# Agent attention and a maxout layer on one core: 2900 operations listed in another order

## The chip, the core and the metric

The kernel runs on one core of one Trainium2 chip. A core has five engines that each run their own instruction stream in order: TensorE (PE in the profile; its weight loads are shown apart as PEld), VectorE (DVE), ScalarE (ACT), GpSimd (POOL) and SyncE (SP), which here issues the DMA transfers. The engines wait for each other through semaphores. The metric is the device time of one execution in microseconds (us).

## The reference

Four batches of 12544 tokens with 128 channels go through an attention over 49 "agents", and the result through a maxout layer of width 768:

```python
def _attn_ref(q, k, v, agents):            # q, k, v: 4 x 12544 x 128; agents: 4 x 49 x 128
    a2k = sm(agents, k)                    # sm: softmax of scale * a @ b.T
    agent_v = a2k @ v                      # 49 x 128 for each batch
    q2a = sm(q, agents)
    return q2a @ agent_v

def _moe_ref(x, w1, w2, w3, w_out):        # x: 50176 x 128; w1, w2, w3: 128 x 768
    h = np.maximum(np.maximum(x @ w1, x @ w2), x @ w3)
    return h @ w_out                       # w_out: 768 x 128
```

Inputs and output are float32; 78.7 MB are read and 25.7 MB are written.

## The kernel before

**What is computed, and how.** The maximum of the three products is rewritten as p1 + max(p2 - p1, max(p3 - p1, 0)) with differences of weights, so that two products have to be formed per slice, and p1 goes into a linear part. For each batch the softmax over the keys gives 49 weighted values (`avT`), and their products with the weight differences give a tile `G` of 49 rows per batch. A group of 1024 queries (there are 49 groups, `s` = 0 to 48; 12 for each batch and one with the rests) then needs: its transposed queries (`qt` on TensorE and `qe` on VectorE, or `qd`, a DMA transpose, for the groups in `TURNED`), its scores (`sc`, L541), their exponentials on ScalarE (`ex`, L547), and for each of six slices `f` of the width 768 two hidden products (`u` and `v`, L566). ScalarE applies a relu to `u` (`a`, L579) and VectorE takes the maximum with `v` (`x`, L582); for `f` = 4 both are in the same PSUM tile, and ScalarE does both steps (L573, L576). Two output tiles `o` = 0, 1 collect a linear part (`li`, L595) and six products (`p`, L604); VectorE scales them (`ov`, L611) and SP stores them (`st`).

**Keys and values.** Batch 0 is worked off first, in 12 pieces of the keys (`kl0.g`) and values (`vl0.g`): load, cast (`kc` on POOL, `vc` on ScalarE), turn on TensorE (`kt`), copy (`ke`), scores (`ks`), exponentials (`kx`), totals (`to`) and values (`kv`). When all are in, `rc0` and `nr0` form `avT`, and `gp`/`gv` the first `G`. No hidden product can start before. The pieces of batches 1 to 3 are spread over the query groups before them; their keys are turned by DMA transposes issued by SP (`kt1.g` to `kt3.g`, L462), as are the queries of `qd`.

**Who decides the order.** A function `graph` names 2900 operations with engine, tiles and predecessors. The text `ORDER` (from L662 on) lists all of them, in one line of words such as `u.3.5/2`: the operation and the slot of each new tile. Each engine executes its own operations in the order of this list; an operation also waits for the operations that it reads from and for the last user of the slot that it takes over. The number of slots is fixed: 3 for the hidden products (`UV`, two PSUM banks each), 2 for the smaller PSUM tiles (`OM`, one bank), 13 for loads (`LD`), 3 each for the casts `QB` and `KB` and the transposed `QT` and `KT`, 11 for outputs (`OS`). Ten `wm` operations (L390) are matmuls of the identity that nothing reads.

**Modes of TensorE.** `graph` gives each TensorE operation one of three modes: `u` and `v` run as two matmuls side by side on 49 rows each (ROW), `sc` and the `G` products as two on 64 columns each (COL), everything else on the full array (FULL):

```python
add(f"u.{s}.{f}", PE, em.hidden(s, f, C31, True), mm(...), mode=ROW, ...)
add(f"sc.{s}", PE, em.q_scores(s), mm(...), mode=COL, ...)
def add(self, name, eng, fn, cost, mode=FULL, ...)
```

In the list of before, after the first hidden product `u.0.1`, TensorE has 1479 operations, and 586 times the mode differs from that of the operation before.

Of the kernel before, what the change touches and what calls it, by code (L numbers as in the profile page):

```python
# [666 lines left out]
to0.6 ke0.9/2 kt0.11/0 ke0.11/0 ks0.11/0 kx0.11/2 vc0.0/0 vd0.11 to0.11 kv0.11 ke0.1/0 ks0.1/2 kx0.1/2 kt0.4/0 kl0.3/7 vl0.8/8
ke0.2/0 vl0.4/6 ks0.10/2 kv0.0 to0.1 vc0.9/0 ks0.9/1 kx0.9/0 kc0.8/2 ke0.4/1 kt0.8/0 vc0.6/1 vl0.3/10 sc.0/1 ke0.8/2 ks0.8/0
wm.2/1 to0.9 kv0.5 kv0.9 vl0.1/2 vc0.10/2 ks0.2/1 kx0.2/0 kx0.8/1 lw3a/9 lw1a/3 kv0.6 lw1b lw2a/12 lw3b lw2b ex.0/0 ks0.4/1
kc0.3/2 kt0.3/0 to0.8 ql.1/7 qc.1/0 lwo/0 cwo kx0.4/3 to0.4 to0.2 kv0.2 vc0.8/1 kx0.10/0 vc0.4/3 ke0.3/1 ks0.3/0 to0.10 kv0.8  # L670
# [213 lines left out]
```

## Time and profile before

| | us |
|---|---|
| median of 3 runs | 443.36 |
| lowest, highest | 443.36, 444.09 |
| span of the profiled execution | 440.9 |
| TensorE busy in the span | 421.0 |
| ScalarE busy | 392.4 |
| VectorE busy | 390.6 |
| GpSimd busy | 169.3 |
| issue to landing, loads of queries, keys, values (median) | 6.8, 8.3, 9.7 |

The profiled execution is told by its span, from the first to the last instruction, alone; the median of the runs is 2.5 us longer, which is what lies around the span. In the rows of the profile a line such as `L566` is a line of the kernel, the tile names stand as out<-in, and `x1248` counts instructions. A matmul's end is modelled, so starts are compared with starts below. "Idle" is the time that an engine had nothing running, and the name behind `<-` is what ended it. TensorE's granted clock was 0.999 over the span.

### The profile page before, as it was taken

The numbers are of one execution on the slowest core, as the hardware profiler recorded it, in microseconds if no ns is written. First come the engines' busy times: TensorE is split into PE (matmuls) and PEld (weight loads), VectorE is DVE, ScalarE is ACT, GpSimd is POOL, SyncE is SP. The second block draws the span as 40 slices with busy tenths as digits, with TensorE's granted clock in tenths as the row PEclk, the third lists the DMA queues.
The fourth block names the chain that finished last, engine by engine and source line by source line (L and its number), as shares of the span: only waits on it lengthen the run. The fifth ranks groups of instructions, "written<-read, shape, count | busy, mean of one in ns | idle before, by whom it ended". The sixth has DMA issues, their size and how long they took to land.

```text
span 440.9 us, 12824 instructions
## 1 busy us (share of the span) xinstructions
PE 421.0 (95%) x5246; PEld 268.6 (61%) x5246; DVE 390.6 (89%) x495; ACT 392.4 (89%) x461; POOL 169.3 (38%) x176
## 2 busy tenths in 40 slices
PE   2678999999999999999999999999999999999997
PEld 2564565666666665666666666665665655656676
DVE  2236998999999999999999989989999999999996
ACT  2269999999998999999999999999999999999983
POOL 3541556667295413480746345634403102000000
PEclk9999999999999999999999999999999999999999
DMA  8999999999999999999999999999987952462144
GB/s 323 409 410 384 347 297 335 315 390 266 399 352 239 297 316 352 273 279 307 419 410 259 242 279 381 268 290 304 277 253 214 246 138 76 117 207 58 49 165 173
DMA packets 99157, 122.50 MB, mean 278 GB/s; under 512 B 72535, under 2 KB 75291, under 8 KB 99099
## 3 DMA queue, kind: packets, MB, share of 16 engines
q1 hardware_dynamic: 98752, 121.46, 92.2%
q8 instruction: 41, 0.67, 0.6%
q10 hardware_dynamic: 347, 0.23, 0.2%
q14 instruction: 17, 0.14, 0.1%
HBM read 78.74 MB, written 25.69 MB: 237 GB/s over the span
## 4 chain that ended last, share of the span: by engine, by line
PE 74%; DMA 15%; ACT 3%; POOL 3%; SPq 2%; DVE 1%; issue 1%; DVEq 0%; ACTq 0%; POOLq 0%
PE UV L566 31%; PE OM L604 28%; DMA LD<-in_k_dram 8%; PE OM L595 5%; PE OM L541 3%; DMA LD<-in_q_dram 2%; ACT AS L579 2%; DMA LD<-in_moe_w_dram 2%; DMA LD<-in_v_dram 2%; PE OM L384 2%; PE OM L531 2%; PE OM L367 2%; DMA KT<-KB 1%; SPq L333 1%; POOL KB L343 1%
## 5 line engine op out<-in xcount | busy, mean ns | idle before, releaser
L582 DVE TENSOR_TENSOR R<-UV,AS 128x1024 bf16<-128x1024 f32 x245 | 293.1, 1218 | 17.2 <-PE UV L566 13.2
L579 ACT ACTIVATE AS<-UV 128x1024 bf16<-128x1024 f32 x245 | 246.1, 1025 | 16.9 <-PE UV L566 13.3
L566 PE MATMUL UV<-EQ,G 49*128 49x512 bf16 (+1 forms) x1248 | 182.6, 369 | 1.0 <-DVE G L456 0.2
L604 PE MATMUL OM<-wo_bf,R 128*128 128x128 bf16 x2340 | 178.3, 220 | 0.0
L604 PEld LDWEIGHTS <-R 128*128 128x128 bf16 x2352 | 139.3, 98 | 41.1 <-issue 38.6
L566 PEld LDWEIGHTS <-G 49*128 49x128 bf16 x1248 | 60.4, 93 | 63.6 <-issue 23.3
L525 POOL CAST QB<-LD 128x1024 bf16<-128x1024 f32 x49 | 50.6, 1043 | 113.4 <-DMA LD<-in_q_dram 73.5
L611 DVE TENSOR_TENSOR OS<-OM,RC 128x512 f32<-128x512 f32 x98 | 66.8, 681 | 3.0 <-PE OM L604 2.0
L343 POOL CAST KB<-LD 128x1152 bf16<-128x1152 f32 (+2 forms) x45 | 50.0, 1120 | 48.7 <-DMA LD<-in_k_dram 32.0
L573 ACT ACTIVATE UV<-UV 128x1024 f32<-128x1024 f32 x49 | 49.9, 1018 | 2.6 <-PE UV L566 1.6
L576 ACT ACTIVATE R<-UV 128x1024 bf16<-128x1024 f32 x49 | 50.2, 1024 | 1.4 <-PE UV L566 0.6
L343 POOL CAST VB<-LD 128x1152 bf16<-128x1152 f32 (+1 forms) x33 | 37.5, 1141 | 26.2 <-PE OM L553 13.6
L595 PE MATMUL OM<-G,EQ 128*128 128x256 bf16 x195 | 37.8, 275 | 0.0
L482 POOL TENSOR_TENSOR EA<-EA,EK 128x441 f32<-128x441 f32 x27 | 27.7, 1026 | 19.1 <-ACT EK L373 18.4
L547 ACT ACTIVATE EQ<-OM 128x512 bf16<-128x512 f32 x49 | 29.5, 603 | 1.2 <-PE OM L541 1.1
L355 DVE COPY KT<-UV 128x1152 bf16<-128x1152 bf16 (+1 forms) x12 | 8.3, 701 | 15.8 <-PE UV L350 13.5
L595 PEld LDWEIGHTS <-EQ 128*128 128x128 bf16 x196 | 12.3, 97 | 15.7 <-issue 15.2
L341 ACT ACTIVATE VB<-LD 128x1152 bf16<-128x1152 f32 (+1 forms) x12 | 12.3, 1040 | 9.9 <-DMA LD<-in_v_dram 9.6
L367 PEld LDWEIGHTS <-KT 128*128 128x128 bf16 x392 | 14.6, 98 | 9.1 <-issue 5.1
L541 PE MATMUL OM<-QT,agT 128*64 128x512 bf16 (+1 forms) x104 | 19.9, 388 | 0.0
L384 PEld LDWEIGHTS <-VB 128*128 128x128 bf16 x392 | 14.0, 96 | 7.3 <-issue 5.6
L373 ACT ACTIVATE EK<-OM 128x441 bf16<-128x441 f32 (+1 forms) x33 | 18.0, 546 | 0.4 <-PE OM L553 0.3
(71 smaller groups left out, 193.3 us busy)
## 6 DMA issues: line engine op xcount, KB each, us to landing
LD<-in_q_dram SPq DMA_DIRECT2D x48, 512.0 KB, 6.8
out_dram<-OS SPq DMA_DIRECT2D x48, 512.0 KB, 5.1
LD<-in_k_dram SPq DMA_DIRECT2D x40, 576.0 KB, 8.3
LD<-in_v_dram SPq DMA_DIRECT2D x40, 576.0 KB, 9.7
LD<-in_v_dram SPq DMA_DIRECT2D x3, 512.0 KB, 8.0
LD<-in_k_dram SPq DMA_DIRECT2D x3, 512.0 KB, 11.2
LD<-in_moe_w_dram SPq DMA_DIRECT2D x6, 192.0 KB, 8.6
KT<-KB SPq DMA_TRANSPOSE x33, 6.6
```

The costliest lines, as they stand in the source:

```text
L343: (self.nc.gpsimd if eng == POOL else self.nc.vector).tensor_copy(out=out, in_=src)
L525: return lambda: self.nc.gpsimd.tensor_copy(out=self.t[f"qb.{s}"], in_=self.t[f"q.{s}"][:, :GT, :])
L541: self.nc.tensor.matmul(self.t[f"qs.{s}"][h * H:(h + 1) * H, jj * P:(jj + pairs) * P], self.agT[:, b, :], self.t[f"qT.{s}"][:, 2 * jj + h: ...
L547: return lambda: self.nc.scalar.activation(self.t[f"e.{s}"], self.t[f"qs.{s}"], AF.Exp, scale=SCALE)
L566: self.nc.tensor.matmul(t[:, h, jj * P:(jj + pairs) * P], self.t[f"G{b}"][h * H:h * H + A, c + f * P:c + (f + 1) * P], self.t[f"e.{s}"][h ...
L573: return lambda: self.nc.scalar.activation(self.t[f"u.{s}.{f}"], self.t[f"u.{s}.{f}"], AF.Relu)
L576: return lambda: self.nc.scalar.activation(self.t[f"r.{s}.{f}"], self.t[f"u.{s}.{f}"], AF.Relu)
L579: return lambda: self.nc.scalar.activation(self.t[f"a.{s}.{f}"], self.t[f"u.{s}.{f}"], AF.Relu)
L582: return lambda: self.nc.vector.tensor_tensor(out=self.t[f"r.{s}.{f}"], in0=self.t[f"v.{s}.{f}"], in1=self.t[f"a.{s}.{f}"], op=ALU.max)
L595: self.nc.tensor.matmul(out[:, c:c + 2 * C], self.t[f"e.{s}"][:, j // 2 * P:(j // 2 + 1) * P], self.t[f"G{of[j // 2]}"][:, C1O:C1O + 2 * C ...
L604: self.nc.tensor.matmul(out[:, c:c + C], self.t[f"r.{s}.{f}"][:, j % 2, j // 2 * P:(j // 2 + 1) * P], self.wo_bf[:, f, :], start=False, st ...
L611: self.nc.vector.tensor_tensor(out=self.t[f"os.{s}"][:, j:j + n, :], in0=self.flat(f"o.{s}.{o}")[:, :n * C].rearrange("p (j c) -> p j c", ...
```

## The change

Only the text `ORDER` is replaced. The operations, their engines, tiles, slots and numbers stay; each engine issues as many instructions as before. What moves:

- **TensorE**: the same 1479 operations after `u.0.1`, in another interleaving of `u`, `v` and `p`; the mode now changes 605 times. The ten `wm` stand among the first 17 TensorE operations; they stood among the last 31 before `u.0.1`, but for one.
- **SP, start**: the loads of batch 0 come in another sequence. In both lists the same 24 loads of keys and values and one of queries (13.4 MB) stand ahead of the six loads of `w1`, `w2`, `w3`.
- **SP, later**: loads and DMA transposes are listed further ahead. Between a transpose of keys and the scores that read it stand, in the median, 81 TensorE operations where there were 19; for queries 81 where there were 40. Where a transpose stands so early, it takes over its slot right behind the last reader (`kt3.3` behind `ks3.0`). Some stores come later and in groups: six of them (`st.29` to `st.24`) now stand between `qd.42` and `qd.41`.
- **POOL**: casts of queries are listed right behind the transpose that frees their slot (`qc.31` behind `qd.27`).

```diff
 ORDER = """
-kl0.10/0 kc0.10/0 kl0.5/1 kl0.0/2 kc0.5/1 prep kt0.10/0 kt0.5/1 kc0.0/0 kt0.0/2 ke0.0/0 ke0.10/1 kl0.7/3 vl0.7/4 vc0.7/0 kl0.6/5
...
-wm.9/2 wm.6/1 kx0.3/1 to0.3 wm.1/0 su.0/1 re.0/0 wm.7/1 ql.2/6 qc.2/1 vd0.10 kv0.4 wm.4/1 rc0/0 vc0.3/1 d31a wm.3/0 vl1.0/5 kv0.3
-kv0.10 vc0.1/0 kv0.1 cw1 wm.8/0 nr0/0 gpa/0 gva wm.5/1 kl1.0/2 d21a kc1.0/2 gpc/2 gvc kl1.1/10 u.0.1/0 a.0.1/0 d31b d32 gpb/1 d21b
...
-sc.24/0 v.23.3/2 x.23.3/0 ex.24/0 v.23.1/1 u.23.2/0 x.23.1/4 a.23.2/1 li.22.1/1 p.22.1.5 kc3.0/0 kt3.0/1 ks3.0/0 kx3.0/1 p.22.1.0
...
-qc.41/2 qd.41/1 ql.47/8 p.38.0.3 p.38.0.1 ov.38.0/0 v.39.4 x.39.4/2 p.38.1.0 qc.47/2 v.39.5/1 x.39.5/9 u.40.1/0 a.40.1/0 p.38.1.4
...
+kl0.2/0 kl0.9/1 wm.0/0 kl0.0/2 ql.0/3 kl0.10/4 kl0.5/5 kc0.0/0 kc0.9/1 prep kt0.9/0 vl0.6/6 ke0.9/0 wm.7/1 wm.6/2 ks0.9/0
+kx0.9/0 wm.8/1 vl0.11/7 kl0.6/8 wm.5/2 vc0.11/0 qc.0/0 kc0.6/1 wm.3/1 wm.9/2 vl0.10/9 vc0.6/1 vc0.10/2 vd0.10 vl0.9/10 wm.1/0
...
+kx0.4/2 ks0.1/0 to0.4 kv0.4 kx0.1/0 vc0.3/3 vc0.1/2 to0.1 rc0/0 kv0.3 lw1a/12 kv0.1 lw3a/11 d31a lw1b cw1 nr0/0 gpa/0 gva lw2a/6
+d21a lw3b d31b lw2b d32 gpc/2 gvc u.0.1/0 a.0.1/0 gpb/1 ql.1/9 qc.1/0 d21b gpd/2 gvb u.0.5/1 a.0.5/1 gvd v.0.1/0 x.0.1/0 u.0.3/2
...
+p.22.0.3 ov.22.0/3 u.23.1/2 a.23.1/0 u.23.2/0 v.23.3/1 a.23.2/1 x.23.3/9 li.22.1/0 p.22.1.4 ks3.0/1 ql.30/3 qd.27/0 ql.31/11
+qc.31/2 kt3.3/2 p.22.1.2 qc.29/0 kc3.4/1 su.24 re.24/1 kx3.0/3 v.23.2/2 x.23.2/2 u.24.5/1 a.24.5/2 v.23.1/0 p.22.1.3 kv3.0
...
+x.38.0/2 li.37.1/1 p.37.1.3 p.37.1.5 u.39.2/2 st.31 st.35 st.32 st.36 st.24 a.39.2/1 v.38.1/0 x.38.1/10 p.37.1.2 u.39.0/1
...
+qd.41/0 v.38.3/0 x.38.3/8 st.34 st.37 li.38.1/0 p.38.1.5 u.39.4/2 a.39.4 v.40.2/1 x.40.2/6 u.39.5/0 p.38.1.4 a.39.5/0 p.38.0.3
...
 """
```

More of the change, by code (lines that the diff above doesn't have):

```diff
@@ L667 @@
[L667 to L670, printed above, removed]
@@ new lines @@
+vl2.7/2 su.13 u.13.3/0 v.12.2/1 x.12.2/0 p.11.1.1 kx2.1/2 qc.19/1 ea2.1 kv2.1 re.13/2 vc2.4/3 va2.1 u.12.0/2 p.11.1.2 a.13.3/2
+p.11.1.5 p.11.1.3 ov.11.1 a.12.0/0 u.13.4/0 a.13.4 v.12.0/1 x.12.0/1 u.13.5/2 li.12.0/1 qt.14/0 qe.14/2 a.13.5/1 p.12.0.3
+p.12.0.4 v.13.4 x.13.4/5 u.13.1/1 a.13.1/0 v.13.5/2 p.12.0.0 x.13.5/9 p.12.0.1 p.12.0.5 p.12.0.2 ov.12.0/7 sc.14/0 u.13.0/0
+v.13.3/2 x.13.3/7 ex.14/2 a.13.0/1 u.13.2/1 li.12.1/1 p.12.1.3 ks2.2/0 p.12.1.5 p.12.1.0 kx2.2/3 a.13.2/2 kt2.5/2 ql.20/12
@@ new lines @@
+va2.5 ov.15.1 a.16.0/1 u.17.4/0 a.17.4 v.16.2/2 x.16.2/0 u.17.5/1 a.17.5/2 ea2.4 vc2.8/2 vc2.10/3 kc2.10/2 ea2.5 li.16.0/0
+p.16.0.5 qt.18/1 qe.18/1 kt2.8/2 v.17.4 x.17.4/5 st.12 st.2 kl3.2/10 kl3.0/12 qc.22/2 kc3.0/0 v.16.0/2 x.16.0/6 p.16.0.2
+p.16.0.4 sc.18/1 v.17.5/1 x.17.5/7 ex.18/1 u.17.3/0 a.17.3/1 p.16.0.1 p.16.0.3 p.16.0.0 ov.16.0/6 u.17.2/2 a.17.2/0 v.17.3/0
+x.17.3/1 u.17.1/1 a.17.1/2 li.16.1/1 ks2.6/0 kx2.6/3 ea2.6 v.17.2/2 x.17.2/9 p.16.1.1 p.16.1.5 v.17.1/0 x.17.1/4 u.17.0/1
+a.17.0/1 su.18 kv2.6 re.18/1 kt2.9/0 va2.6 p.16.1.4 vc2.9/0 u.18.5/2 a.18.5/0 p.16.1.0 v.17.0/1 x.17.0/6 vl3.3/1 u.18.3/0
@@ new lines @@
+x.19.0/0 u.20.5/2 a.20.5/1 v.20.5/1 x.20.5/8 li.19.0/0 p.19.0.5 p.19.0.4 sc.21/1 ex.21/1 v.20.1/2 x.20.1/3 u.20.3/0 p.19.0.3
+p.19.0.0 p.19.0.2 a.20.3/2 u.21.3/1 p.19.0.1 ov.19.0/2 li.19.1/1 a.21.3/1 u.20.4/0 v.20.3/2 x.20.3/2 p.19.1.1 ks2.9/0 p.19.1.2
+a.20.4 kx2.9/3 ea2.9 fo2/0 u.20.2/1 a.20.2/0 v.20.4 x.20.4/6 su.21 kv2.9 vc3.0/0 kc3.5/2 vc3.2/2 qc.26/1 ql.29/10 ql.27/11
+qd.26/2 va2.9 p.19.1.3 re.21/1 v.20.2/2 x.20.2/7 u.20.0/1 p.19.1.5 p.19.1.4 li.20.0/0 p.19.1.0 ov.19.1 u.21.5/0 a.20.0/2
@@ new lines @@
+p.24.0.0 ks3.2/1 kx3.2/1 ea3.2 p.24.0.4 ov.24.0/9 u.25.2/1 a.25.2/0 v.25.3/2 v.25.4 x.25.4/3 x.25.3/8 kv3.2 va3.2 li.24.1/0
+p.24.1.0 v.25.2/1 x.25.2/1 p.24.1.2 u.25.0/2 a.25.0/2 v.25.1/0 su.26 re.26/0 p.24.1.3 u.26.5/1 a.26.5/0 li.25.0/1 x.25.1/2
+p.25.0.4 u.26.1/2 v.26.5/0 x.26.5/7 a.26.1/1 u.26.4/1 a.26.4 p.25.0.2 p.24.1.4 p.24.1.5 p.24.1.1 ov.24.1 u.26.3/2 a.26.3/0
+v.25.0/0 x.25.0/4 p.25.0.5 sc.27/0 ex.27/1 vc3.6/2 kt3.5/0 v.26.4 x.26.4/5 v.26.3/2 p.25.0.1 ks3.3/0 kx3.3/0 ea3.3 p.25.0.0
+x.26.3/6 p.25.0.3 ov.25.0/2 u.27.5/0 a.27.5/2 u.26.2/1 v.26.1/2 x.26.1/9 su.27 kv3.3 va3.3 re.27/1 vl3.7/3 vc3.7/1 li.25.1/1
@@ new lines @@
+st.15 x.28.1/5 u.28.2/1 a.28.2/1 li.27.1/1 p.27.1.5 qt.30/0 p.27.1.2 qe.30/0 u.29.3/2 a.29.3/0 v.28.0/0 x.28.0/4 p.27.1.3
+li.28.0/0 p.28.0.4 v.28.2/1 u.29.5/2 a.29.5/2 x.28.2/8 p.27.1.0 p.27.1.1 p.27.1.4 ov.27.1 p.28.0.1 v.29.5/0 u.29.4/2 a.29.4
+u.29.1/1 a.29.1/1 x.29.5/0 p.28.0.3 p.28.0.2 vc3.8/3 p.28.0.0 p.28.0.5 ov.28.0/7 sc.30/1 qd.33/0 ex.30/1 v.29.3/0 v.29.4
+x.29.4/1 x.29.3/6 v.29.1/1 x.29.1/10 ks3.6/0 su.30 li.28.1/1 p.28.1.3 kt3.9/2 kx3.6/2 u.29.0/0 a.29.0/0 u.30.3/2 a.30.3/1
+p.28.1.2 kv3.6 va3.6 re.30/1 p.28.1.1 v.29.0/1 x.29.0/5 u.29.2/0 p.28.1.5 li.29.0/0 p.28.1.0 p.28.1.4 a.29.2/2 v.29.2/2 x.29.2/2
@@ new lines @@
+v.32.4 a.32.5/1 x.32.4/3 v.32.5/2 x.32.5/8 u.32.1/0 a.32.1/0 p.31.0.0 p.31.0.2 p.31.0.5 ov.31.0/8 sc.33/1 u.32.2/1 v.32.1/2
+x.32.1/10 ex.33/1 v.32.2/0 a.32.2/1 x.32.2/4 li.31.1/0 p.31.1.0 p.31.1.1 p.31.1.4 ks3.9/1 kx3.9/2 p.31.1.2 u.33.5/1 a.33.5/0
+v.32.3/2 x.32.3/2 su.33 p.31.1.5 u.32.0/0 a.32.0/1 kv3.9 va3.9 re.33/0 p.31.1.3 ov.31.1 u.33.4/1 a.33.4 v.32.0/2 li.32.0/1
+p.32.0.2 p.32.0.5 x.32.0/5 v.33.5/0 x.33.5/0 st.11 ea3.9 fo3/0 v.33.4 x.33.4/1 p.32.0.3 u.33.3/2 a.33.3/1 p.32.0.4 p.32.0.1
@@ new lines @@
+a.41.0/2 u.40.4/2 a.40.4 p.39.0.2 qc.46/2 qc.44/0 qc.48/1 p.39.0.1 p.39.0.4 v.41.2/0 u.40.5/1 a.40.5/0 x.41.2/10 p.39.0.3
+p.39.0.0 ov.39.0/0 v.40.4 x.40.4/7 sc.42/0 st.28 qd.44/1 v.40.5/0 x.40.5/11 u.41.1/1 a.41.1/1 li.39.1/1 p.39.1.1 ex.42/2
+v.41.0/2 x.41.0/0 p.39.1.2 u.40.3/0 a.40.3/0 v.41.1/1 x.41.1/4 p.39.1.0 p.39.1.5 p.39.1.3 su.40/0 re.40/2 u.42.0/2 v.40.3/0
+x.40.3/2 p.39.1.4 ov.39.1 a.42.0/2 u.42.2/1 a.42.2/1 li.40.0/0 p.40.0.2 p.40.0.1 u.41.4/2 a.41.4 v.42.2/0 x.42.2/1 u.41.5/1
+a.41.5/0 p.40.0.3 p.40.0.0 su.41/1 re.41/1 p.40.0.5 p.40.0.4 ov.40.0/7 v.41.4 x.41.4/9 v.41.5/0 x.41.5/3 u.42.1/1 a.42.1/1
@@ new lines @@
+a.45.2/1 p.42.1.5 p.42.1.3 ov.42.1 qd.47/2 st.40 st.42 p.43.0.0 u.44.4/1 a.44.4 v.45.2/0 x.45.2/4 u.44.5/2 p.43.0.1 a.44.5/0
+p.43.0.2 su.44/0 re.44/0 p.43.0.4 p.43.0.3 ov.43.0/6 v.44.4 x.44.4/7 v.44.5/0 x.44.5/1 u.45.1/2 a.45.1/1 li.43.1/1 p.43.1.3
+p.43.1.4 v.45.0/1 x.45.0/3 sc.46/0 ex.46/1 u.44.3/0 a.44.3/0 v.45.1/2 x.45.1/6 p.43.1.5 p.43.1.0 su.45/0 p.43.1.1 re.45/2
+u.46.0/1 a.46.0/2 v.44.3/0 x.44.3/0 p.43.1.2 ov.43.1 u.46.2/2 a.46.2/1 li.44.0/0 p.44.0.2 p.44.0.5 u.45.4/1 a.45.4 v.46.2/0
+x.46.2/5 u.45.5/2 a.45.5/0 p.44.0.0 p.44.0.4 p.44.0.3 p.44.0.1 ov.44.0/3 v.45.4 x.45.4/2 v.45.5/0 st.38 x.45.5/10 li.44.1/1
@@ new lines @@
+p.44.1.1 u.46.1/2 a.46.1/1 sc.47/0 ex.47/0 v.46.0/1 x.46.0/11 p.44.1.5 u.45.3/0 a.45.3/0 v.46.1/2 x.46.1/1 st.43 p.44.1.4
+su.46/0 re.46/1 p.44.1.2 p.44.1.0 u.47.0/1 a.47.0/2 v.45.3/0 x.45.3/7 p.44.1.3 ov.44.1 u.47.2/2 a.47.2/1 li.45.0/0 p.45.0.4
+p.45.0.0 u.46.4/1 v.47.2/0 x.47.2/0 u.46.5/2 a.46.4 a.46.5/0 li.45.1/1 p.45.0.1 p.45.0.3 p.45.0.5 p.45.0.2 ov.45.0/6 v.46.4
+x.46.4/8 u.47.1/0 v.46.5/2 x.46.5/9 st.44 a.47.1/1 p.45.1.1 p.45.1.3 p.45.1.5 v.47.0/1 x.47.0/10 sc.48/0 ex.48/2 v.47.1/2
+x.47.1/6 u.46.3/0 a.46.3/0 p.45.1.4 li.46.0/0 p.46.0.4 p.45.1.2 p.45.1.0 u.47.5/0 a.47.5/2 u.48.2/1 ov.45.1 v.46.3/2 x.46.3/3
@@ L853 @@
+p.47.0.3 p.47.0.4 ov.47.0/3 a.48.4 v.48.4 a.48.3/2 v.48.3/1 x.48.3/5 p.47.1.0 p.47.1.1 x.48.4/8 li.48.0/0 p.48.0.1 p.48.0.2
+p.48.0.5 p.48.0.0 ov.47.1 st.47 p.48.0.4 p.48.0.3 ov.48.0/6 st.48.0 li.48.2/1 li.48.1/1 p.48.1.5 p.48.1.1 p.48.1.3 st.48.1
+p.48.1.2 p.48.1.4 p.48.1.0 ov.48.1 st.48.2 p.48.2.5 p.48.2.4 p.48.2.0 p.48.2.2 p.48.2.3 p.48.2.1 ov.48.2 st.48.3
 """
```

321 lines of the change are left out of this document (140 added, 181 removed).

## The prediction

> **What bounds the kernel now.** I read the page first, then busy time by stretch, then the starts of single matmuls in the timeline, and last the DMA rows. The page's span, TensorE's line and its chain of waits:
>
> ```profile
> span 440.9 us, 12824 instructions
> ...
> PE 421.0 (95%) x5246; PEld 268.6 (61%) x5246; DVE 390.6 (89%) x495; ACT 392.4 (89%) x461; POOL 169.3 (38%) x176
> ...
> PE 74%; DMA 15%; ACT 3%; POOL 3%; SPq 2%; DVE 1%; issue 1%; DVEq 0%; ACTq 0%; POOLq 0%
> ```
>
> The same busy times by stretch (columns: length, then PE, PEld, DVE, ACT, POOL busy with counts, clock, DMA share, GB/s):
>
> ```profile
> 0.00:10.00 10.00, 3.17 (x26) 2.32 (x26) 2.13 (x15) 1.28 (x1) 3.62 (x9) 1.00 0.84 313
> 10.00:20.00 10.00, 5.28 (x58) 3.89 (x59) 3.07 (x5) 3.41 (x6) 5.13 (x6) 1.00 1.03 410
> 20.00:30.00 10.00, 8.23 (x112) 6.57 (x110) 4.96 (x8) 5.69 (x8) 4.35 (x4) 1.00 1.02 409
> 30.00:40.00 10.00, 8.01 (x144) 5.28 (x144) 3.52 (x10) 9.25 (x14) 1.15 (x1) 1.00 1.04 394
> 60.00:430.00 370.00, 369.13 (x4562) 232.73 (x4559) 351.00 (x430) 349.30 (x406) 144.40 (x148) 1.00 0.93 268
> ```
>
> There are two stages. For 40 us batch 0 is loaded, at about 410 GB/s, and no compute engine is full. After that TensorE is busy for 369.13 of 370 us, while VectorE and ScalarE have 19 and 21 us free. A busy PE may hide waits, so the starts decide (first column: start):
>
> ```profile
> 260.38 1.15 PE L566 MATMUL UV<-EQ,G 49*128 49x512 bf16 x6
> 261.47 0.40 PE L604 MATMUL OM<-wo_bf,R 128*128 128x128 bf16 x4
> ...
> 264.14 1.07 PE L604 MATMUL OM<-wo_bf,R 128*128 128x128 bf16 x16
> 265.14 0.88 PE L566 MATMUL UV<-EQ,G 49*128 49x512 bf16 x6
> 265.95 0.84 PE L604 MATMUL OM<-wo_bf,R 128*128 128x128 bf16 x12
> 266.73 0.41 PE L541 MATMUL OM<-QT,agT 128*64 128x512 bf16 x2
> 267.07 0.88 PE L566 MATMUL UV<-EQ,G 49*128 49x512 bf16 x6
> 267.88 0.39 PE L595 MATMUL OM<-G,EQ 128*128 128x256 bf16 x2
> ...
> 268.44 0.61 PE L604 MATMUL OM<-wo_bf,R 128*128 128x128 bf16 x8
> 268.98 0.60 PE L566 MATMUL UV<-EQ,G 49*128 49x512 bf16 x4
> 269.52 0.62 PE L604 MATMUL OM<-wo_bf,R 128*128 128x128 bf16 x8
> ```
>
> From start to next start, 16, 12 and 8 matmuls of `p` take 1.00, 0.78 and 0.54 us. Four more cost 0.22 to 0.24, so a `p` operation is about 0.223 us and each of these runs has about 0.10 us on top (0.78 - 3 x 0.223 = 0.11; 0.54 - 2 x 0.223 = 0.09). That extra stands wherever the next operation has another mode. The back-to-back sequence shows no idle at all here: TensorE is the bound, and its time is its work plus mode changes plus what it really waits.
>
> It does wait a little. In the first row above six hidden matmuls took 1.09 us where 0.81 is usual. The rows of the two other engines at that place:
>
> ```profile
> 259.49 1.22 DVE L582 TENSOR_TENSOR R<-UV,AS 128x1024 bf16<-128x1024 f32 x1
> 260.07 1.02 ACT L576 ACTIVATE R<-UV 128x1024 bf16<-128x1024 f32 x1
> ```
>
> VectorE ended at 260.71 and ScalarE at 261.09, each releasing a `UV` slot that a hidden product was waiting for. Comparing all matmul starts with the usual step between the same two kinds of operation, I find 52 such waits of over 0.06 us, 7.4 us together; the first and the last are in these rows:
>
> ```profile
> 43.39 0.71 PE L566 MATMUL UV<-EQ,G 49*128 49x512 bf16 x4
> ...
> 416.30 1.02 PE L566 MATMUL UV<-EQ,G 49*128 49x512 bf16 x6
> ```
>
> **Part 1, mode changes.** The list of before changes mode 586 times after `u.0.1`, the new one 605 times: 19 more, at 0.10 us, +1.9 us. All of it is on the path, since TensorE has nothing to overlap it with. Bounds: the `sc` pair took 0.34 us (266.73 to 267.07), 0.12 above the 0.215 of its columns, so 19 x 0.12 = 2.3 above; below, 0.09 from the x8 run gives 1.7. I take 1.9. The matmuls themselves are the same 1479 operations, at zero.
>
> [...]
>
> **Part 2, waits for `UV` slots.** How long a slot is taken, from two pieces of the chain of waits in order of time (start, length), and what ScalarE and VectorE wait for in all (us, times, longest):
>
> ```profile
> 41.72 0.41 PE UV L566 x2
> 42.15 1.56 ACT AS L579 x2
> ```
>
> ```profile
> DVE R L582 <- PE UV L566: 12.9, 34, 0.7
> ACT AS L579 <- PE UV L566: 12.6, 40, 0.6
> ```
>
> ScalarE starts 0.43 us after the product, so a slot that ScalarE frees is back after 0.43 + 1.02 = 1.45 us, one that VectorE frees after 0.43 + 1.22 = 1.65. I counted, with the durations above, how much TensorE work is listed between a product and the next user of its slot. Too short are 21 slots behind ScalarE and 18 behind VectorE in the old list, 4.9 us missing altogether; in the new one 21 and 16, 4.8 us. So -0.1. The rest, 7.4 - 4.9 = 2.5 us, comes from queues on the two engines: the share of stretches of 10 us in which an engine is given more than 10 us of work is 23% for ScalarE and 30% for VectorE before, 21% and 32% after, and the mean overload of the two together falls from 0.22 to 0.19 us. Scaled, -0.3. Together -0.4. Bounds: all 2.5 us gone (-2.6), or as much again (+2.4).
>
> **Part 3, the start.**
>
> ```profile
> 31.17 8.14 DMA LD<-in_moe_w_dram
> ...
> 36.30 2.23 ACT L341 ACTIVATE VB<-LD 128x1152 bf16<-128x1152 f32 x2
> 38.90 0.84 ACT L410 ACTIVATE w_bf<-LD 128x768 bf16<-128x768 f32 x1 [0.37 <-DMA LD<-in_moe_w_dram]
> ...
> 40.27 0.39 PE L566 MATMUL UV<-EQ,G 49*128 49x512 bf16 x2
> ```
>
> The last cast of values ends at 38.53 and the first hidden product follows at 40.27; a load of `w` issued at 31.17 lands only at 39.31. Both lists put the same 13.4 MB ahead of `w`, in one queue that is already full, so no sequence of them ends earlier unless the queue runs better: 30 to 40 us at 410 in place of 394 GB/s would give 10 x 16/410 = -0.4. Against that, the new list waits for slots in other places (13 `LD` slots, three `KB`); one load held up costs its own share of the queue, 0.59 MB/410 GB/s = +1.4. I take 0, since the loads that need an old slot have it freed by casts well before their turn in the queue. The warm-up matmuls at 0.38 us each lay in TensorE's free time (8.01 of 10 us busy at 30 to 40) and cost nothing there; nothing comes from their move, as the clock column is 1.00 from the first stretch on, where they hardly ran. The end of the list has the same dependencies in both (`u.48` to `ov.48.2`), at zero.
>
> **Part 4, transposes, loads, stores, casts.** Rows of the DMA issues and of POOL's longest wait behind a transpose:
>
> ```profile
> out_dram<-OS SPq DMA_DIRECT2D x48, 512.0 KB, 5.1
> ...
> KT<-KB SPq DMA_TRANSPOSE x33, 6.6
> ...
> QT<-QB SPq DMA_TRANSPOSE x29, 5.3
> ...
> POOL QB L525 <- DMA QT<-QB: 32.2, 8, 9.2
> ```
>
> In the old list the median transpose of keys stands 19 TensorE operations ahead of its reader, about 5 us; in the new one 81, about 20 us, against 6.6 us to landing. That is safer, but TensorE had hardly a wait for a transpose to lose, so it is worth 0. SP now stands behind `ks` and `sc` for `KT` and `QT` slots, with loads queued behind it, and POOL behind transposes (it did so for 32.2 us before, at no cost). Loads have a median of 194 TensorE operations to the scores that need them, so this is hidden too. The tightest place is `qd.41`: it needs the slot that `sc.40` frees, and six stores stand just ahead of it in SP's queue, 6 x 0.52 MB/410 GB/s = 7.7 us of transfers. `sc.39`, which lets SP go on, and `sc.41`, which reads the result, are 14 us of TensorE work apart; less 7.7 for the stores and some 5.3 for the two transposes this leaves about 1 us. At zero, with +2 as the upper end.
>
> **Sum.** 440.9 + 1.9 - 0.4 + 0 + 0 = 442.4 us of span. With the 2.5 us by which the median of the runs exceeds the profiled span, 444.9; I say 444.8, 0.3% above 443.36.
>
> **Rivals.**
> - *The slot waits shrink more than the modes cost (faster).* One mechanism: the new interleaving of `u`, `v` and `p` keeps ScalarE and VectorE from queueing behind each other, so that TensorE's 7.4 us of slot waits fall. For it: both engines have 5% free, and the overload of VectorE falls from 0.110 to 0.086 us per stretch. Against it: the number of too short slots is equal in both lists. It decides once waits fall by more than 1.9 + 0.9 = 2.8 us, to under 4.6. With the waits halved and the better queue of part 3: 443.36 + 1.9 - 3.7 - 0.4 = 441.2.
> - *Nothing that can be told.* The extra modes fall at places where TensorE would have waited for a slot anyway. Half of the 1.9 us would have to lie there: 443.36 + 0.9 - 0.4 = 443.9. For it speaks that waits and changes both cluster around the hidden products; against, that 52 waits are few beside 605 changes.
> - *Supply becomes the bound (slower by more).* SP, held behind `sc` for a `QT` slot, and the stores behind it make `qd.41` and its neighbours late. It begins where the 1 us of part 4 is used up; two or three such places at 2 us each give 444.8 + 2 to 6, about 448. Against it: 20 us of lead elsewhere.
> - *The order makes more of the queues on ScalarE and VectorE (slower)*: waits grow by the 2.4 us of part 2, 447.2; this is the upper end of the forecast's own range.
>
> **How the numbers follow.** What a measurement of this kernel can tell from no change is 0.2%, 0.9 us. Chances: forecast, modes paid and waits about as before, 0.46; waits shrink, 0.25; nothing to tell, 0.21; supply, 0.08. Slower by over 0.2% is the forecast and supply, 0.54; same 0.21; faster 0.25. The forecast's own range is 444.3 to 447.2. The whole range reaches down into the faster case, to 441.2, which leaves out about 0.09, and up to 447.3, which leaves out most of supply and a little more, about 0.1.
>
> **What would show it.** Right: runs of `p` and `u` in the timeline with the same steps but more of them alternating, TensorE busy for all but some us from 41 us on, idle of L579 and L582 behind `PE UV L566` between 50 and 430 us not under the 12.6 and 12.9 us of part 2, the first hidden product between 39.9 and 41.7. What would make the prediction wrong: steps at mode changes well under 0.10, slot waits under 4.6 us, a first hidden product before 39.5, or TensorE waiting for `QT`, `KT` or a cast.

## The result, and the profile after

The changed kernel takes 446.96 us (median; 446.09 to 448.31) against 443.63 us for the kernel before on the same chip: a ratio of 1.0073, 95% interval 1.0051 to 1.0096. It is slower by 3.3 us where the forecast had 1.4. The profiled execution has a span of 444.6 us against 440.9. The page of after, with the clock line of its 40 slices:

```profile
span 444.6 us, 12850 instructions
...
PE 421.9 (95%) x5246; PEld 265.8 (60%) x5246; DVE 391.8 (88%) x495; ACT 392.6 (88%) x461; POOL 169.2 (38%) x176
...
PEclk9988899999999999999999999999999999999999
...
PE 85%; ACT 5%; DVE 4%; DMA 3%; issue 2%; POOL 1%; SPq 0%; ACTq 0%; DVEq 0%; POOLq 0%
```

The busy times look like those of before. The clock line does not: TensorE's clock is cut in the third to fifth slice. By stretch (columns as in the prediction; the clock is the third number from the end), after:

```profile
20.00:30.00 10.00, 6.47 (x108) 5.10 (x106) 2.71 (x7) 6.99 (x11) 3.94 (x4) 0.87 1.02 410
30.00:40.00 10.00, 7.46 (x156) 6.01 (x154) 5.57 (x10) 7.95 (x11) 2.29 (x2) 0.95 1.03 395
38.00:41.00 3.00, 1.62 (x24) 0.93 (x24) 2.44 (x9) 2.60 (x5) 0.00 (x0) 1.00 1.09 371
41.00:48.00 7.00, 6.66 (x40) 2.79 (x38) 5.05 (x7) 4.71 (x7) 4.05 (x4) 0.51 1.03 400
60.00:430.00 370.00, 369.05 (x4550) 230.44 (x4547) 351.02 (x426) 348.42 (x406) 143.43 (x146) 1.00 0.93 266
```

and before, for the two stretches that the prediction had not looked at:

```profile
38.00:41.00 3.00, 2.59 (x33) 1.17 (x31) 2.88 (x9) 2.51 (x5) 0.00 (x0) 1.00 1.10 370
41.00:48.00 7.00, 6.51 (x62) 3.52 (x60) 6.69 (x9) 6.60 (x10) 3.64 (x4) 1.00 1.03 402
```

From 41 to 48 us TensorE is busy for 6.66 and 6.51 of the 7 us, but after has 40 matmuls there and before 62, at a granted clock of 0.51 in place of 1.00. Just ahead of it, from 38 to 41 us, TensorE was busy for 1.62 us after and 2.59 us before; that is where the warm-up matmuls stood. From 60 to 430 us the clock is 1.00, and after starts 12 matmuls fewer in the same time.

Where the 3.5 us by which TensorE ends later come from can be summed from the starts. For each kind of TensorE operation I took the usual time to the next start (with and without a change of mode; the value that 15% of its steps lie below, over the traces of the table) and called the rest excess. Times in us; the kernels below the first two are those of the experiments; the columns and the last operation's 0.3 add up to TensorE's end:

| kernel | mode changes | first hidden product | usual steps | excess up to 60 us | excess later | TensorE's end |
|---|---|---|---|---|---|---|
| before | 586 | 40.27 | 379.39 | 1.50 | 16.37 | 437.80 |
| after | 605 | 40.88 | 381.85 | 2.85 | 15.41 | 441.26 |
| w_both | 605 | 40.35 | 381.16 | 2.16 | 15.92 | 439.87 |
| h_ab | 585 | 40.91 | 379.92 | 2.93 | 17.29 | 441.34 |
| x1_more_modes | 624 | 42.45 | 382.99 | 1.32 | 16.92 | 443.96 |
| x2_fewer_modes | 533 | 40.97 | 374.40 | 2.58 | 47.83 | 466.05 |
| fewer_waits | 587 | 40.66 | 379.62 | 1.84 | 24.12 | 446.52 |
| banks_kept | 590 | 40.59 | 380.55 | 1.55 | 16.71 | 439.68 |

After against before: the first product +0.61; up to 60 us, at half the clock, +1.35 of excess and +0.69 in usual steps (five operations that occur only there, which the column takes as they ran: 381.85 against 381.16 in w_both); mode changes +1.77; waits later -0.96. Together +3.46.

The steps at mode changes are those of before. Timeline of after (first column: start):

```profile
264.79 0.61 PE L604 MATMUL OM<-wo_bf,R 128*128 128x128 bf16 x8
265.33 0.93 PE L566 MATMUL UV<-EQ,G 49*128 49x512 bf16 x6
266.20 1.07 PE L604 MATMUL OM<-wo_bf,R 128*128 128x128 bf16 x16
267.20 0.95 PE L566 MATMUL UV<-EQ,G 49*128 49x512 bf16 x6
```

Eight matmuls of `p` and a change take 0.54 us, sixteen and a change 1.00, as before.

### The profile page after: what moved, and what is told of

It is laid out like the page before. It is cut to its first block, busy times and chain, and to the rows that moved or that the text cites. A ratio compares the mean times of both kernels' runs of the same rounds, so it can differ in the third digit from the quotient of the medians.

```text
span 444.6 us, 12850 instructions
## 1 busy us (share of the span) xinstructions
PE 421.9 (95%) x5246; PEld 265.8 (60%) x5246; DVE 391.8 (88%) x495; ACT 392.6 (88%) x461; POOL 169.2 (38%) x176
## 4 chain that ended last, share of the span: by engine, by line
PE 85%; ACT 5%; DVE 4%; DMA 3%; issue 2%; POOL 1%; SPq 0%; ACTq 0%; DVEq 0%; POOLq 0%
PE UV L566 34%; PE OM L604 31%; PE OM L595 6%; PE OM L541 4%; PE OM L384 2%; DVE R L582 2%; DMA LD<-in_k_dram 2%; PE OM L531 2%; ACT AS L579 2%; PE OM L367 2%; PE OM L553 1%; ACT VB L341 1%; DMA ag_st<-in_agents_dram 1%; PE UV L350 1%; ACT EK L373 1%
## 5 line engine op out<-in xcount | busy, mean ns | idle before, releaser
L582 DVE TENSOR_TENSOR R<-UV,AS 128x1024 bf16<-128x1024 f32 x245 | 293.5, 1219 | 18.3 <-PE UV L566 12.9
L579 ACT ACTIVATE AS<-UV 128x1024 bf16<-128x1024 f32 x245 | 245.7, 1026 | 18.1 <-PE UV L566 15.4
L566 PE MATMUL UV<-EQ,G 49*128 49x512 bf16 (+1 forms) x1248 | 185.0, 371 | 1.3 <-DVE G L456 0.3
L604 PE MATMUL OM<-wo_bf,R 128*128 128x128 bf16 x2340 | 181.5, 220 | 0.0
L566 PEld LDWEIGHTS <-G 49*128 49x128 bf16 x1248 | 58.8, 93 | 64.7 <-issue 24.4
L373 ACT ACTIVATE EK<-UV 128x441 bf16<-128x441 f32 (+1 forms) x12 | 5.9, 504 | 15.2 <-PE UV L367 15.1
L384 PE MATMUL OM<-EK,VB 128*128 128x49 bf16 x392 | 17.7, 186 | 1.4 <-DVE KR L431 0.7
L373 ACT ACTIVATE EK<-OM 128x441 bf16<-128x441 f32 (+1 forms) x33 | 18.0, 547 | 0.9 <-PE OM L367 0.6
```

Of the source, the lines that this page charges most:

```text
L384: self.nc.tensor.matmul(out, vb[:, j, :], e[:, j * A:(j + 1) * A], start=False, stop=True, skip_group_check=True)
L566: self.nc.tensor.matmul(t[:, h, jj * P:(jj + pairs) * P], self.t[f"G{b}"][h * H:h * H + A, c + f * P:c + (f + 1) * P], self.t[f"e.{s}"][h ...
L579: return lambda: self.nc.scalar.activation(self.t[f"a.{s}.{f}"], self.t[f"u.{s}.{f}"], AF.Relu)
L582: return lambda: self.nc.vector.tensor_tensor(out=self.t[f"r.{s}.{f}"], in0=self.t[f"v.{s}.{f}"], in1=self.t[f"a.{s}.{f}"], op=ALU.max)
L604: self.nc.tensor.matmul(out[:, c:c + C], self.t[f"r.{s}.{f}"][:, j % 2, j // 2 * P:(j // 2 + 1) * P], self.wo_bf[:, f, :], start=False, st ...
```

## The experiments

**Warm-ups moved back (e1_warm_back) and moved away (e2_warm_front).** The first is after with eight of its `wm` back between `kv0.4` and `gpc`; the second is before with eight of its `wm` among the first operations:

```diff
 e1_warm_back, from after
-kx0.9/0 wm.8/1 vl0.11/7 kl0.6/8 wm.5/2 ...
-... to0.4 kv0.4 kx0.1/0 vc0.3/3 vc0.1/2 to0.1 rc0/0 kv0.3 lw1a/12 kv0.1
+... to0.4 kv0.4 wm.9/1 wm.6/2 kx0.1/0 vc0.3/3 vc0.1/2 to0.1 wm.1/1 wm.7/2 wm.4/1 rc0/0 kv0.3 wm.3/2 lw1a/12 kv0.1 wm.8/1
 e2_warm_front, from before
-prep kt0.10/0 kt0.5/1 kc0.0/0 kt0.0/2 ke0.0/0 ke0.10/1
+prep wm.9/1 wm.6/2 wm.1/1 kt0.10/0 kt0.5/1 wm.7/2 kc0.0/0 kt0.0/2 ke0.0/0 ke0.10/1 wm.4/2 wm.3/0 wm.8/2 wm.5/0
```

> The order of after, with eight of its ten warm-up matmuls taken from the first 17 TensorE operations and listed again between kv0.4 and gpc, where TensorE waits for the last values. Theory A (the warm-ups' move costs clock): the granted clock, 0.50 from 41.2 to 48.0 us in after, stays at 1.00 there; 25 fewer matmuls were started from 41 to 48 us than before, at some 0.085 us each about 2.1 us, so the time falls from 447.0 to about 444.9. Theory B (the clock was low where TensorE waited for other engines anyway, and mode changes and slot waits make up the whole 3.3 us): the time stays within 0.5 us of 447.0, whatever the clock.

> The order of before, with eight of its warm-up matmuls taken from ahead of the first hidden product and listed among the first TensorE operations, between prep and kt0.6. Theory A: the clock falls to about 0.5 for one or two pieces of 3 to 7 us near 40 us, and the time rises from 443.6 to between 444.5 and 446. Theory B: no more than 0.4 us above 443.6, even if the clock falls. If the clock stays at 1.00 here, TensorE's other work in these 10 us suffices and the warm-ups alone are not the cause in after.

Measured: e1_warm_back 444.77 us against 443.23 (ratio 1.0047, 1.0027 to 1.0067), e2_warm_front 445.03 against 443.23 (1.0043, 1.0029 to 1.0056). The stretch from 40 to 50 us of e1_warm_back, and that of e2_warm_front:

```profile
40.00:50.00 10.00, 9.32 (x83) 4.44 (x84) 9.36 (x14) 9.59 (x14) 5.38 (x6) 1.00 1.05 396
```

```profile
40.00:50.00 10.00, 9.14 (x62) 4.07 (x59) 7.71 (x13) 7.54 (x12) 5.26 (x6) 0.66 1.03 399
```

The eight matmuls, which nothing reads, decide the clock in both directions, and with it 1.8 us each way. Theory A holds, theory B falls. The price is somewhat under the 2.1 us expected, an estimate that had counted 25 fewer matmuls from 41 to 48 us where the two rows above show 22; at its own 0.085 us each that is 1.9.

But single executions of e1_warm_back lay between 443.8 and 452.4 us. The profile of a late execution of e1_ab, a variant of it with the later order of before, points to the reason.

**The two halves exchanged (h_ba, h_ab, e1_ab).** Three lists join one order up to `u.2.2` (61 us in before, 64 in after; the expectations had put it at 57) with the other behind it; operations that the first part lacks come at the joint.

```diff
 h_ba: before up to u.2.2, then after
 ... x.2.1/8
-u.2.2/2 v.2.3/1 li.1.1/1 vc1.1/2 kv1.1 ...
+kt1.1/0 ks1.1/0 su.2 kx1.1/0 kl1.3/4 ql.4/1 qc.4/2 kc1.3/2 vc1.1/1 ...
 h_ab: after up to u.2.2, then before   (e1_ab: the same behind e1_warm_back)
 ... qc.5/1 kx1.1/1
-u.2.2/1 v.2.3/2 li.1.1/0 kx1.1/3 ea1.1 kv1.1 p.1.1.0 ...
+u.2.2/1 v.2.3/2 li.1.1/0 kv1.1 p.1.1.1 a.2.2/0 ...
```

> The order of before up to u.2.2 (some 57 us), then the rest in the order of after: 606 mode changes after u.0.1 in place of 586, with the clock and the start of before. Theory A (modes at 0.10 us, slot waits about equal): 20 x 0.10 = +2.0, bounds 1.2 to 2.2 with the waits, so 444.8 to 445.8 against 443.6. Theory C (the start and the clock are the whole loss): 443.4 to 444.0.

> The order of after up to u.2.2, then the rest in the order of before: 585 mode changes after u.0.1, one fewer than before, with the start of after. Theory A: the first hidden product comes 0.6 us later than before and half a clock costs 2.1 us, so 443.6 + 2.7 - 0.1 = 446.2, at least 445.2. Theory B: 443.5 to 444.3, the start lost nothing.

> The order of e1_warm_back up to u.2.2, then the rest in the order of before: 585 mode changes in place of 605, same start and same clock as e1_warm_back. Theory A (what e1_warm_back still loses to before, 1.5 us, is mode changes): 444.8 - 20 x 0.096 = 442.9, at most 443.6. Theory D (it is the start, a later first product): no change from 444.8, at least 444.3.

Measured: h_ab 446.63 us against 443.23 (1.0088, 1.0067 to 1.0108), near the 446.2 of theory A, so theory B falls: with the start of after, and one mode change fewer than before, it is as slow as after. Its clock is that of after:

```profile
41.00:48.00 7.00, 6.66 (x40) 2.79 (x40) 5.08 (x7) 4.64 (x7) 4.06 (x4) 0.51 1.03 399
```

By the table the 20 fewer mode changes save it 1.93 us against after, and later waits take 1.88 back; behind another start the order of before waits more than in its own place (17.29 against 16.37 us). So this run alone would not show the price of the mode changes; x1_more_modes below does. The other join, h_ba, took 448.02 us, more than any theory had. Its timeline shows an accident of the joint:

```profile
61.96 0.39 PE L595 MATMUL OM<-G,EQ 128*128 128x256 bf16 x2
64.53 0.41 PE L384 MATMUL OM<-EK,VB 128*128 128x49 bf16 x9 [2.18 <-POOL VB L343]
```

POOL had been given the casts of `q.4` and `k1.3`, just loaded, ahead of the values that `kv1.1` needs; TensorE waited for 2.18 us, and then ran at half clock (0.50) from 65.1 to 68.6 us as well. Less the wait it would take 445.8 us, and less half of those 3.4 us as well 444.1; this estimate spans both theories, so the run is no clean test of the mode changes. It does show the forecast's supply rival in action, only not in the kernel that was forecast.

e1_ab took 445.46 us (1.0061, 1.0033 to 1.0088), with 12 executions from 443.96 to 452.01; its lowest is no lower than the 443.84 of e1_warm_back, so 20 fewer mode changes show no gain here, and neither theory A nor D is settled by it. Its profiled execution is a late one (span 450.2, first product at 44.77 us). Key transposes of nine matmuls in its timeline, and the clock column of the same time:

```profile
32.97 1.14 PE L350 MATMUL UV<-ident,KB 128*128 128x128 bf16 x9
36.07 0.66 PE L350 MATMUL UV<-ident,KB 128*128 128x128 bf16 x9
```

```profile
20.00:36.00 16.00, 12.59 (x154) 9.61 (x154) 5.07 (x9) 8.51 (x13) 6.36 (x6) 1.00 1.02 409
```

The same nine matmuls take 1.14 us up to 34 us and 0.66 us from 36 us on: TensorE ran at about half speed (0.66/1.14 = 0.58) until some 35 us, although the column says 1.00. In e2_warm_front nine such transposes take 1.17 us at 21.3 us, and there the column does say 0.50:

```profile
13.40:23.60 10.20, 8.30 (x84) 6.62 (x84) 3.72 (x5) 4.03 (x7) 5.77 (x6) 0.50 1.03 407
```

In after, whose warm-ups stand in front, the transposes are fast from 16.4 us on, but for a piece from 27.5 to 30.9 us:

```profile
10.42 1.14 PE L350 MATMUL UV<-ident,KB 128*128 128x128 bf16 x9 [4.32 <-POOL KB L343]
...
16.36 0.68 PE L350 MATMUL UV<-ident,KB 128*128 128x128 bf16 x9 [1.15 <-POOL KB L343]
```

So the new place of the warm-ups is good for something: it brings the clock up early (the first record of the clock begins at 13.8 us in after, at 23.7 in before). That holds for the start order of after; in e2_warm_front the clock came up at 10 us too, but fell again at 13.4. What after lacks is a second set before the first product.

**Both sets (w_both), and three more only (w_three).**

```diff
-SPARE = 10
+SPARE = 18
-... to0.4 kv0.4 kx0.1/0 ... to0.1 rc0/0 kv0.3 lw1a/12 kv0.1 ... gpa/0
+... to0.4 kv0.4 wm.10/1 wm.11/2 kx0.1/0 ... to0.1 wm.12/1 wm.13/2 wm.14/1 rc0/0 kv0.3 wm.15/2 lw1a/12 kv0.1 wm.16/1 ... gpa/0 wm.17/1
 w_three: SPARE = 13, one each behind to0.1, kv0.3, kv0.1
```

> The order of after with its ten warm-up matmuls where they are, and eight more at the places where e1_warm_back had put them (between kv0.4 and gpc). Theory A (clock): the granted clock stays at 1.00 from 41 to 48 us, and the first product comes no later than in after (40.9 us), since the early warm-ups still bring the clock up by 14 us; so the time falls from 447.0 to about 444.8, and single runs stay within 1.5 us of each other, unlike those of e1_warm_back (443.8 to 452.4). Rival (what made runs of e1_warm_back late is something other than the missing early warm-ups): the same spread as there.

> As w_both, but with three more warm-ups only, one each behind to0.1, kv0.3 and kv0.1. Theory A with a threshold: in after TensorE was busy for about 1.8 of the 3.4 us before the clock fell at 41.2 us; three warm-ups add 0.6, to 2.4 us, or 70%, where before had 76 to 82% from 34 to 40 us and kept its clock. If that is enough, 444.8 as for w_both; if not, the clock is 0.50 from 41 to 48 us and the time 446.5 to 447.

Measured: w_both 444.94 us against 443.07 (1.0042, 1.0028 to 1.0055), its executions between 444.73 and 445.52; w_three 445.10 (1.0046, 1.0029 to 1.0064), 444.10 to 446.74. From 40 to 50 us, w_both and w_three:

```profile
40.00:50.00 10.00, 9.12 (x83) 4.44 (x82) 9.36 (x15) 9.32 (x14) 5.29 (x6) 1.00 1.05 397
```

```profile
40.00:50.00 10.00, 9.25 (x82) 4.55 (x82) 9.46 (x15) 9.27 (x13) 5.25 (x6) 1.00 1.05 396
```

As theory A had it, the small spread of w_both included. That the late starts come from the missing early warm-ups is likely, and not proved: 8 of the 23 executions without them (e1_warm_back, e1_ab) lay more than 3 us above the lowest of their run and none of the 12 with both sets, but only one late execution has a trace. And it holds for the start order of after alone: before has no early set either, and only one of its 66 executions lay so far up. Three matmuls, 0.6 us of work, keep the clock up from 40 to 50 us in the profiled execution as eight do; the mean clocks of 0.987 and 0.988 in the two longest executions of w_three, like the 0.988 of after, suggest that in these they were not enough.

w_both is also the cleanest comparison for the rest. It starts as early as before (40.35 against 40.27 us) and at full clock, and ends 2.07 us later: +0.08 start, +1.77 for 19 mode changes, +0.66 up to 60 us, whose cause I did not separate, and -0.45 later. The later part holds a new wait of 0.82 us that after had hidden behind its late start:

```profile
80.80 0.38 PE L384 MATMUL OM<-EK,VB 128*128 128x49 bf16 x8 [0.82 <-POOL VB L343]
```

**The price of a mode change (x1_more_modes, x2_fewer_modes, x3_runs_merged).** All from before, with TensorE operations moved by a few places:

```diff
 x1_more_modes, one of 21 moves
-p.8.0.3 p.8.0.4 p.8.0.0 a.9.1/1 sc.10/0 ex.10/0
+p.8.0.3 p.8.0.4 a.9.1/1 sc.10/0 p.8.0.0 ex.10/0
 x2_fewer_modes (p and li only)
-li.18.1/1 p.18.1.2 p.18.1.1 p.18.1.4 u.19.0/1 a.19.0/2 v.19.2/0 x.19.2/8 kv2.8 va2.8 u.20.5/2 a.20.5/1 p.18.1.5
+li.18.1/1 p.18.1.3 p.18.1.4 u.19.0/1 a.19.0/2 v.19.2/0 x.19.2/8 kv2.8 va2.8 u.20.5/2 p.18.1.1 p.18.1.0 p.18.1.5
 x3_runs_merged (u and v too)
-v.19.1/0 x.19.1/3 u.19.2/1 a.19.2/0 v.19.3/2 x.19.3/1
+v.19.3/2 u.19.2/1 v.19.1/0 x.19.1/3 a.19.2/0 x.19.3/1
```

> The order of before, with 21 p operations of groups 2 to 46 moved by one to three TensorE operations so that they part pairs of hidden products: 624 mode changes after u.0.1 in place of 586, no UV slot taken earlier or later than its turn. Theory A: 38 x 0.096 = +3.6 us (bounds 3.4 to 4.6 by the price range of the forecast), so 446.8 against 443.2. Rival (half of the changes fall where TensorE would have waited for a slot anyway): +1.8, 445.0.

> The order of before, in which p and li operations alone are moved among the other TensorE operations so that runs of one mode get longer: 533 mode changes in place of 586, and the slots listed too short fall from 4.9 to 3.2 us. Theory A: 53 x 0.096 = -5.1 us for the modes and up to -1.7 for the slots, so 438.1, between 436.4 and 439.5. Rival: longer runs of hidden products make slot waits that take the gain, at least half of it: 440.7 or more.

> As x2_fewer_modes, with the hidden products u and v and the sums moved too: 481 mode changes in place of 586, too short slots 1.6 us. Theory A: 105 x 0.096 = -10.1, and up to -3.3 for slots, so 433.1 or less. Rival: VectorE and ScalarE, with 19 and 21 us free in the 370 us from 60 to 430, are offered their work less evenly, and what TensorE waits for them rises by more than half of the gain: 438 or more.

Measured: x1_more_modes 447.19 us against 442.96 (1.0094, 1.0076 to 1.0111): +4.2, where theory A had 3.6 (3.4 to 4.6) and the rival 1.8. In the table its usual steps are 3.60 above before, 0.095 for each of the 38 changes. The price stands, and none of it is seen to be hidden.

x2_fewer_modes took 471.11 us (1.0642, 1.0618 to 1.0665) and x3_runs_merged 559.28 us (1.2611, 1.2580 to 1.2643). The modes did pay in x2_fewer_modes: its usual steps are 4.99 us below before, 0.094 for each of 53. But its excess grew by 32.5 us. The largest of TensorE's own waits behind the other engines (us, times, longest; they count idle time alone, and so only a part of it):

```profile
PE UV L566 <- DVE R L582: 7.4, 19, 0.8
...
PE UV L566 <- ACT R L576: 5.3, 12, 0.7
...
PE OM L595 <- DVE OS L611: 4.5, 6, 1.4
```

Before has none of these in this view. Longer runs of hidden products take the three `UV` slots faster than ScalarE and VectorE return them, and then starve both: from before to x2_fewer_modes VectorE's wait for hidden products (L582) grows from 13.2 to 22.5 us, ScalarE's (L579) from 13.3 to 21.8. The rival was right, by far more than the half that it had claimed. My count of slots listed too short had said 1.7 us less waiting: taken one slot at a time, it does not see queues.

**Fewer waits (fewer_waits, banks_kept).** From before, with TensorE, VectorE and ScalarE operations behind `u.0.1` moved so that the waits, summed over all three queues with the durations of the traces, fall:

```diff
 fewer_waits
-sc.20/1 ex.20/2 ... v.19.1/0 x.19.1/3 u.19.2/1 a.19.2/0 v.19.3/2 x.19.3/1 ks2.8/0 kx2.8/3 li.18.1/1
+sc.20/0 v.19.1/2 ex.20/2 ... x.19.1/3 u.19.2/1 v.19.3/0 a.19.2/0 x.19.3/1 ks2.8/1 li.18.1/0 p.18.1.0 ... kx2.8/3
 banks_kept
+sc.20/0 v.19.1/0 ex.20/2 ... x.19.1/3 v.19.3/1 u.19.2/2 a.19.2/0 x.19.3/1 li.18.1/1 p.18.1.2 p.18.1.4 ks2.8/0 kx2.8/3
```

> The order of before up to u.0.1; after that TensorE, VectorE and ScalarE operations are moved, and UV and OM slots handed out anew, so that with the durations of this case's traces TensorE waits 1.5 us less, at 587 mode changes (586 before). Theory A (the time is work, plus 0.096 us for each mode change, plus waits for slots): 443.1 - 1.4 = 441.7, at least 441.0 and at most 442.5, under both kernels. Rival (waits that the durations do not show, for copies, casts and transposes, take the gain): 442.6 to 444.

> As fewer_waits (the order of before up to u.0.1, after that TensorE, VectorE and ScalarE operations moved for fewer waits), but the sums su and re of a group and the pieces ks, kx, kv of keys and values that share its PSUM tile are counted as one chain in the order of the list, which fewer_waits had left out; by the durations of this case's traces TensorE then waits 1.6 us less than in before, at 590 mode changes (+0.4). Theory A (the 9 us that fewer_waits lost are waits within these shared tiles): 443.1 - 1.2 = 441.9, at most 442.7. Rival (other waits outside the count): above 443.1.

Measured: fewer_waits 452.09 us against 443.07 (1.0206, 1.0185 to 1.0228), banks_kept 444.20 against 443.45 (1.0013, 0.9995 to 1.0031). What ScalarE waits for from 100 to 300 us, fewer_waits and then before:

```profile
ACT EK L373 <- PE OM L553: 3.0, 4, 1.3
ACT EK L373 <- DVE RC L558: 1.8, 1, 1.8
```

```profile
ACT EK L373 <- PE OM L553: 0.3, 1, 0.3
```

The exponentials of a key piece (L373) read a PSUM tile that the sums of a group (L553, L558) share; moved past each other, they wait, for 4.8 us in these rows. With such waits counted, 8 of the 9 us are back. The expected gain is not: excess later is 16.71 against 16.37 before. None of these lists beats the kernel before.

## Why the prediction was right or wrong

- **What bounds the kernel**: right. TensorE is busy for 369.05 of 370 us from 60 to 430, and its chain share rose to 85%.
- **Part 1, mode changes**: right. Forecast +1.9 at 0.10 each; +1.77 in w_both, and 0.093 to 0.095 each in w_both, x1_more_modes and x2_fewer_modes. What TensorE does in that time no row shows; its length alone was measured.
- **Part 2, slot waits**: right in sign and about in size, in part by luck. Forecast -0.4; the excess later is -0.96 in after and -0.45 in w_both. The way there was weaker than its result: the same count misled by over 30 us in x2_fewer_modes. The mark set for it held for one engine only; from 50 to 430 us of after:

```profile
ACT AS L579 <- PE UV L566: 13.1, 36, 0.9
```

```profile
DVE R L582 <- PE UV L566: 11.1, 31, 0.9
```

ScalarE is above its 12.6, VectorE below its 12.9, and the time still rose.

- **Part 3, the start**: this step failed. It put the move of the warm-ups at nothing and said that "nothing comes from their move, as the clock column is 1.00 from the first stretch on, where they hardly ran". The warm-ups had held the clock up, and without them it was 0.51 from 41 to 48 us. With a set there again, w_both starts 0.53 us earlier than after and gains 1.38 us up to 60 us (0.69 in usual steps, 0.69 in excess); 0.5 is given back later by the wait for a cast of values. Net 1.4 in the profiles, 1.5 by the medians against before (3.3 - 1.9), and 1.8 in e1_warm_back. The column was misread: it shows 1.00 also where no change of the clock has been recorded yet, and in before the first record begins at 23.7 us. The rows of before itself tell it apart, nine key transposes in 1.17 us and later in 0.66, so its clock came up only by some 24 us:

```profile
20.78 1.17 PE L350 MATMUL UV<-ident,KB 128*128 128x128 bf16 x9
...
26.68 0.66 PE L350 MATMUL UV<-ident,KB 128*128 128x128 bf16 x9
```

- **Part 4, transposes, loads, stores**: right. In after no idle time of TensorE is left from 50 to 430 us, so none behind a transpose, load or store. (The 194 operations of lead are those of the key loads in the new list; the loads of queries have 164.) Not foreseen was a late cast of values, 0.82 us in w_both.
- **Sum**: 444.9 by the parts. With what after's profile shows instead, -0.1 for the modes, -0.6 for the waits, +0.6 for the start and +2.0 up to 60 us, of which 1.4 is the clock, it is 446.8, against 446.96 measured. That this lies within the forecast's own range, up to 447.2, is luck: the upper end was set by slot waits that grow by 2.4 us, and they fell. What filled the room was the clock, which had no term and no rival.
- **Rivals**: the slot waits fell by under 1 us where 2.8 were needed, no mode change is seen to be hidden, and supply held TensorE up by 2 us in h_ba only. None of them was the clock.

## What to carry to other kernels

Before calling a matmul that nothing reads free, look at how busy TensorE is in the few microseconds ahead of its dense stage (from 38 to 41 us 1.62 us in after, with a clock of 0.51 from 41 us on, and 2.59 in before, with 1.00), and compare durations of equal matmuls there: the clock column alone does not show a clock that was never up (1.00 in before where nine transposes took 1.17 us in place of 0.66). When an order is judged, price mode changes at their measured step (0.093 to 0.095 us here), but replay waits through all queues and shared tiles together; counting slots one at a time promised 1.7 us and cost over 30.

## What the hardware did that I had not expected

- **The clock fell although TensorE was not idle.** In the nine places where a profile of after or of the runs (x3_runs_merged not counted) shows the clock fall between 24 and 66 us, TensorE had been busy for 1.2 to 2.1 of the last 3.4 us (1.29 and 1.77 at 27.5 and 41.1 us in after; 1.84 at 27.2 in w_three; 2.06 at 46.3 in e1_ab). In before it was never under 2.16 there, and no fall is recorded. That is no safe limit: x3_runs_merged has a fall at 453.6 us behind 2.21.
- **The clock moved in pieces of 3.4 us**: it was low for 3.4 us (27.5 to 30.9 in after), 6.9 (41.1 to 48.0) and 10.3 (46.3 to 56.6 in e1_ab). In each trace all recorded changes lie whole pieces apart (the two falls in after four: 41.15 - 27.49 = 13.66 us, 3.41 for each piece). A stretch of 3.4 us as little busy as 1.27 us, at 24.1 in w_both and 25.1 in e1_warm_back, passed without a fall. Counted in these pieces, it lies across two with 2.21 and 2.12 us in e1_warm_back, which would explain that. In w_both it leaves a piece of 1.62 us, less than the 1.77 behind which after lost its clock:

```profile
23.85:27.26 3.41, 2.21 (x39) 1.59 (x39) 1.04 (x3) 2.22 (x4) 0.56 (x1) 1.00 1.01 403
27.26:30.67 3.41, 2.12 (x46) 1.85 (x45) 0.75 (x2) 3.41 (x6) 2.24 (x3) 1.00 1.03 416
```

```profile
25.58:28.99 3.41, 1.62 (x37) 1.41 (x36) 0.26 (x2) 3.41 (x7) 1.67 (x2) 1.00 1.03 415
```

So the busy time of a piece does not decide alone; what else does stays open.

- **One nearly busy piece did not bring it back**: in after TensorE was busy for 3.06 of 3.40 us from 41.1 on, and the clock stayed at half for as long again:

```profile
41.10:44.50 3.40, 3.06 (x19) 1.27 (x18) 2.31 (x4) 2.66 (x4) 1.87 (x2) 0.51 1.05 398
44.50:48.00 3.50, 3.50 (x24) 1.52 (x21) 2.64 (x4) 1.95 (x4) 2.19 (x2) 0.50 1.03 408
```

Here, too, busy time does not decide alone. In w_three a piece with 2.87 us brought the clock back, and in e1_ab one with 3.41 did not:

```profile
27.25:30.66 3.41, 2.87 (x41) 2.64 (x41) 0.43 (x1) 3.26 (x6) 2.59 (x3) 0.50 1.02 412
30.66:34.07 3.41, 3.04 (x65) 2.48 (x63) 1.79 (x3) 1.71 (x4) 1.96 (x2) 1.00 1.02 411
```

```profile
49.69:53.10 3.41, 3.41 (x20) 1.16 (x20) 2.30 (x4) 1.93 (x3) 1.04 (x1) 0.50 1.01 405
53.10:56.52 3.42, 3.42 (x22) 1.42 (x19) 2.95 (x3) 2.70 (x5) 0.88 (x1) 0.50 0.26 105
```
